# Turning the queries of one batch by DMA instead of on TensorE, and moving a VectorE reduction to an earlier step, in a sparse attention and gated feed-forward kernel

## The chip, the cores and the metric

The kernel runs on one core of a Trainium2 chip. The metric is the time of one execution on the device in microseconds (us), lower is better. Engines: PE is TensorE (PEld its weight loads), DVE is VectorE, ACT is ScalarE, POOL is GpSimd, SP is SyncE, which here only issues transfers. Each execution also reports the mean clock that was granted to PE, as a share of full speed.

## The reference, cut to what matters

Four batches of attention (8 heads, 768 tokens, head size 64). A query sees its neighbours within 16 tokens and one summary of each block of 32 keys: the elementwise maximum of the keys, and the mean of the values. The result, 3072 tokens of width 512, goes through a gated feed-forward layer.

```
k_sum = k.reshape(B, H, nb, 32, D).max(axis=3)
v_sum = v.reshape(B, H, nb, 32, D).mean(axis=3)
scores_l = where(|i - j| < 16, q @ k.T / sqrt(D), -1e9)
scores_s = q @ k_sum.T / sqrt(D) + log(32)
x = softmax([scores_l, scores_s]) @ [v, v_sum]          # 3072 x 512
out = x + sigmoid(x @ w_res) * ((gelu(x @ w_gate) * (x @ w_val)) @ w_out)
```

## The kernel before

The work is cut into eight units of half a batch (384 tokens), 0 to 7; unit u belongs to batch u // 2. A unit has two stretches. In the first, twelve "fo steps" each compute one 128-row slice of the hidden layer: four g matmuls and four vv matmuls on PE, a GELU on ACT, a product gvT on DVE. The second is the output part (r and f matmuls), and PE starts it with the scores s of the *next* unit; their exp runs on ACT, the mask product on DVE (P), and PE's ao matmuls need the masked P. So at the end of a unit ACT, DVE and PE hand work to each other at close quarters.

Batch data for the next batch are prepared in the shadow of the fo steps. For batches 2 and 3, q and k are loaded token by token (`q_nat`, `k_nat`) and turned to head-by-token order by a transposing DMA (`turn_q`, `turn_k`). For batch 1, q was loaded in another order (`q_sb`, four tokens to a partition) and turned on PE, with a copy by ACT, in eight `q_step`s. The maxima over key blocks (`k_blocks`) are DVE work for every batch. POOL copies the block means of v into place (`vsum_bc`).

```python
def load_q(b, half):                      # 4 tokens to a partition: 96 x 8 runs
    t = qk.tile([QP, H, QJ, D], BF16, tag=f"q_sb{half}", name="q_sb")
    nc.gpsimd.dma_start(out=t.rearrange("p h j d -> p h (j d)"), in_=q[b, :, ...])

def load_q_nat(b):                        # token order: 6 transfers of 128 x 8 runs
    for c in range(NQ):
        nc.gpsimd.dma_start(out=q_nat[:, c]..., in_=q[b, :, c * 128:(c + 1) * 128, :]...)

def turn_q(b, half):
    cs = slice(half * NSUB, (half + 1) * NSUB)
    nc.sync.dma_start_transpose(out=qT[b % 2][:, cs]..., in_=q_nat[:, cs]...)

def k_blocks(b, hp):
    kw = kW[b % 2][:, :, hp]
    ks = work.tile([128, NB], BF16, tag="ks", name="ks")
    nc.vector.tensor_reduce(out=ks..., in_=kw[:, :, 0:QT]..., axis=X, op=ALU.max)       # L205
    nc.vector.tensor_copy(kw[:, :, BAND:BAND + NB], ks....to_broadcast([128, NT, NB]))  # L209

def vsum_bc(b, lo, hi, eng):              # called four times with three tiles each, on POOL
    eng.tensor_copy(vext[b % 2][96:128, lo:hi, :, 0:D], src)                            # L263

# ... (cut) the main loop, u = unit, nb = next batch, half = u % 2
for fo in range(...):
    fo_step(st, gvT, fo)
    if u == 0 and fo >= 8:
        q_step(0, 1, fo - 8, ps_t, "t")
    if u == 2 and fo < NP:
        q_step(1, 1, fo, ps_t, "t")
    # ... (cut)
    if half == 1 and nb < B:
        # ... (cut)
        if fo == (4 if nb == 1 else 1):
            vsum_grp(nb, ps_t, "t")
            for i in range(4):
                vsum_bc(nb, 3 * i, 3 * i + 3, nc.gpsimd)
            if nb > 1:
                turn_q(nb, 0); turn_q(nb, 1)
        if nb == 1:
            if fo < NP:
                k_step(nb, fo, ps_t, "t")
            elif 7 <= fo < 7 + NP:
                q_step(nb, 0, fo - 7, ps_t, "t")
        elif 8 <= fo < 8 + NP:
            k_blocks(nb, fo - 8)

# the output part, which begins with the scores of unit n = u + 1
def mid_out(u, st, gvT, nst):
    s_step(n, 0, nst); res_step(st, 0); ffn_step(st, gvT, 0, 0, 2)
    s_step(n, 1, nst); ffn_step(st, gvT, 0, 2, 6)
    av_step(n, 0, nst)                    # ao: needs the masked P of s_step(n, 0)
    # ... (cut)
```

The softmax here doesn't subtract the row's maximum and nothing guards it: scores larger than these inputs give would overflow.

## Time and profile before

| | before |
|---|---|
| time, median of 3 | 277.61 us (275.67 to 278.51) |
| the profiled execution | 275.43 us, span of the trace 273.5 us |
| PE busy | 257.3 us, 94% of the span |

The profile page of the kernel before. The first line gives busy time per engine. The second part cuts the span into 40 slices; PEclk is the granted PE clock in tenths. The last line is the start of the part on the chain of work that ended last.

```profile
PE 257.3 (94%) x2280; PEld 138.6 (51%) x2305; DVE 155.3 (57%) x341; ACT 128.6 (47%) x204; POOL 103.4 (38%) x140
...
PE   7889988999989999999979999999989999999994
...
PEclk9999999999999999999999999999999999999999
DMA  5999999999002999949902899969802410130003
...
PE 74%; DMA 11%; DVE 5%; POOL 4%; issue 3%; ACT 1%; POOLq 0%; DVEq 0%
```

PE is the bottleneck: over 90% busy in almost every slice. The slices with a digit below 9 lie in the start-up (to about 48 us), at the ends of units 1, 3 and 5 (slices 11, 20 and 29, counted from 0) and at the very end. DMA is busy throughout until 68 us (slices 0 to 9); after that it has pauses.

PE's waits in the kernel before, longest first (total us, times, longest us):

```profile
PE ao L291 <- DVE P L280: 2.7, 2, 1.6
PE s L273 <- ACT P L277: 1.6, 2, 1.1
```

Both concern the end of units. Where they come from is seen in the timeline. First, the end of unit 1 (columns: start, duration, engine, line, operation, output<-input, shapes, and in brackets the idle time before it and what ended that):

```profile
77.34 0.36 PE L230 MATMUL tp<-ident,q_sb 96*64 96x96 bf16 x8
...
77.64 0.35 PE L273 MATMUL s<-qT,kW 64*128 64x64 bf16 x12
77.75 0.48 ACT L232 COPY qT<-tp 128x384 bf16<-128x384 bf16 x1 [1.11 <-PE tp L230]
...
78.25 1.28 ACT L277 ACT_TABLE_LOAD   x1
...
79.54 0.90 ACT L277 ACTIVATE P<-s,bias_t 128x768 bf16<-128x768 f32 x1
...
80.49 0.29 PE L273 MATMUL s<-qT,kW 64*128 64x64 bf16 x8 [1.10 <-ACT P L277]
```

The last q step stands between the last vv and the scores. ACT's copy of it (0.48 us) comes before the reload of its table (1.28 us), so the exp P starts at 79.54, and the second group of scores, which needs the score buffer, waits 1.10 us.

Second, the end of unit 3 (DVE, POOL and the PE instruction that waited):

```profile
135.72 5.70 POOL L263 COPY vext<-vsum 32x1536 bf16<-32x1536 bf16 x4 [8.34 <-DMA vsum<-vpart]
...
136.91 0.37 DVE L209 COPY kW<-ks 128x288 bf16<-128x288 bf16 x1
...
138.63 1.46 DVE L209 COPY kW<-ks 128x288 bf16<-128x288 bf16 x1
...
141.91 0.23 DVE L209 COPY kW<-ks 128x288 bf16<-128x288 bf16 x1
...
143.19 1.02 DVE L280 TENSOR_TENSOR P<-P,maskt 128x768 bf16<-128x768 bf16 x2
...
143.80 0.38 PE L291 MATMUL ao<-vext,P 128*64 128x65 bf16 x12 [1.61 <-DVE P L280]
```

The key block steps sit between the last gvT products and the mask product P. One of the four copies L209 takes 1.46 us where a later one takes 0.23: it overlaps POOL's four copies L263, which run back to back from 135.72 to 141.42, 1.43 us apart. PE waits 1.61 us for the masked P.

### The profile page before, as it was taken

How to read it: one execution, taken by the hardware profiler on the slowest of the kernel's cores; microseconds unless marked ns; L12 is line 12 of the kernel's file. 1: busy time of each engine (PE TensorE's matmuls, PEld its weight loads, DVE VectorE, ACT ScalarE, POOL GpSimd, SP SyncE). 2: the span in 40 equal slices, each digit the busy share in tenths (PEclk: the TensorE clock that was granted, in tenths of full speed). 3: DMA queues.
4: the chain of work that ended last, by engine and by line, in shares of the span. 5: the costliest groups of instructions: out<-in, count | busy, mean ns of one | idle time of the engine just before them, and what ended most of it. 6: DMA issues, size and time to landing. Idle time of an engine off the chain costs nothing.

```text
span 273.5 us, 5780 instructions
## 1 busy us (share of the span) xinstructions
PE 257.3 (94%) x2280; PEld 138.6 (51%) x2305; DVE 155.3 (57%) x341; ACT 128.6 (47%) x204; POOL 103.4 (38%) x140
## 2 busy tenths in 40 slices
PE   7889988999989999999979999999989999999994
PEld 2445643555544555445634565445634565456543
DVE  5857432499427534665597644665597544764424
ACT  1776346565473555733363436633462437443320
POOL 8795574260340796216160697054520000000000
PEclk9999999999999999999999999999999999999999
DMA  5999999999002999949902899969802410130003
GB/s 88 172 107 188 196 209 201 183 149 172 10 0 46 159 143 133 87 120 134 163 4 43 136 155 132 117 119 154 134 0 49 135 18 2 39 112 25 0 2 115
DMA packets 100074, 28.37 MB, mean 104 GB/s; under 512 B 83912, under 2 KB 97056, under 8 KB 100048
## 3 DMA queue, kind: packets, MB, share of 16 engines
q0 software_dynamic: 63760, 14.87, 60.1%
q1 hardware_dynamic: 36288, 13.14, 23.9%
q8 instruction: 18, 0.29, 0.5%
q14 instruction: 8, 0.07, 0.1%
HBM read 29.36 MB, written 6.29 MB: 130 GB/s over the span
## 4 chain that ended last, share of the span: by engine, by line
PE 74%; DMA 11%; DVE 5%; POOL 4%; issue 3%; ACT 1%; POOLq 0%; DVEq 0%
PE f L365 20%; PE g L317 20%; PE vv L317 19%; PE r L355 6%; DMA w_out<-in_moe_w_out_dram 4%; DMA w_val<-in_moe_w_val_dram 4%; PE ao L291 3%; DMA q_sb<-in_q_dram 3%; PE s L273 2%; DVE ks L205 2%; POOL vext L105 1%; DVE gvT L323 1%; POOL w_gate L182 1%; PE f L389 1%; PE tp L230 1%
## 5 line engine op out<-in xcount | busy, mean ns | idle before, releaser
L323 DVE TENSOR_TENSOR gvT<-ge,vv 128x384 bf16<-128x384 f32 x96 | 52.8, 552 | 62.1 <-PE vv L317 59.5
L322 ACT ACTIVATE ge<-g 128x384 f32<-128x384 f32 x96 | 47.0, 490 | 68.9 <-DVE gvT L323 44.5
L317 PE MATMUL g<-xT,w_gate 128*128 128x384 bf16 x384 | 78.6, 326 | 0.1
L317 PE MATMUL vv<-xT,w_val 128*128 128x384 bf16 x384 | 78.4, 326 | 0.2 <-DVE gvT L323 0.2
L365 PE MATMUL f<-w_out,gvT 128*128 128x512 bf16 x262 | 64.8, 380 | 1.4 <-DMA w_out<-in_moe_w_out_dram 1.0
L317 PEld LDWEIGHTS <-w_val 128*128 128x128 bf16 x384 | 37.5, 98 | 25.5 <-issue 0.8
L317 PEld LDWEIGHTS <-w_gate 128*128 128x128 bf16 x384 | 36.1, 98 | 25.1 <-issue 1.3
L365 PEld LDWEIGHTS <-gvT 128*128 128x128 bf16 x276 | 24.8, 98 | 28.2 <-DMA w_out<-in_moe_w_out_dram 1.5
L277 ACT ACTIVATE P<-s,bias_t 128x768 bf16<-128x768 f32 x32 | 28.8, 901 | 19.8 <-PE s L273 19.2
L105 POOL DMA_DIRECT2D vext<-in_v_dram x48 | 32.9, 745 | 10.8 <-DMA w_out<-in_moe_w_out_dram 4.6
L263 POOL COPY vext<-vsum 32x1536 bf16<-32x1536 bf16 x14 | 20.0, 1464 | 28.7 <-DMA vsum<-vpart 28.6
L280 DVE TENSOR_TENSOR P<-P,maskt 128x768 bf16<-128x768 bf16 x32 | 17.6, 557 | 19.8 <-ACT P L277 18.1
L371 DVE SCALAR_TENSOR_TENSOR th<-th,f 128x512 f32<-128x512 f32 (+1 forms) x25 | 16.5, 660 | 17.5 <-PE f L365 17.2
L358 ACT ACTIVATE th<-r 128x512 f32<-128x512 f32 x24 | 14.2, 595 | 26.1 <-PE r L355 26.0
L355 PE MATMUL r<-w_res,xT 128*128 128x512 bf16 x88 | 23.8, 380 | 1.5 <-issue 1.0
L297 DVE TENSOR_TENSOR xn<-ao,rz 128x384 bf16<-128x384 f32 x32 | 17.8, 557 | 1.3 <-DVE rz L295 0.2
L374 DVE SCALAR_TENSOR_TENSOR o<-th,xn 128x512 f32<-128x512 f32 (+1 forms) x25 | 16.8, 670 | 0.9
L291 PEld LDWEIGHTS <-P 128*64 128x64 bf16 x384 | 8.7, 110 | 16.4 <-issue 6.6
L118 POOL DMA_DIRECT2D k_nat<-in_k_dram x24 | 16.4, 740 | 0.3 <-issue 0.3
L205 DVE TENSOR_REDUCE ks<-kW 128x24 bf16<-128x768 bf16 x16 | 15.1, 942 | 1.5 <-ACT kW L220 1.4
L291 PE MATMUL ao<-vext,P 128*64 128x65 bf16 x384 | 12.1, 199 | 3.5 <-DVE P L280 2.7
L355 PEld LDWEIGHTS <-xT 128*128 128x128 bf16 x96 | 8.8, 98 | 9.2
(71 smaller groups left out, 167.0 us busy)
## 6 DMA issues: line engine op xcount, KB each, us to landing
out_dram<-o SPq DMA_DIRECT2D x23, 256.0 KB, 2.3
vext<-in_v_dram POOLq DMA_DIRECT2D x48, 64.0 KB, 6.2
q_sb<-in_q_dram POOLq DMA_DIRECT2D x4, 384.0 KB, 9.6
w_gate<-in_moe_w_gate_dram POOLq DMA_DIRECT2D x6, 256.0 KB, 9.8
w_val<-in_moe_w_val_dram POOLq DMA_DIRECT2D x6, 256.0 KB, 10.3
w_out<-in_moe_w_out_dram POOLq DMA_DIRECT2D x3, 512.0 KB, 13.0
k_nat<-in_k_dram POOLq DMA_DIRECT2D x24, 64.0 KB, 4.3
q_nat<-in_q_dram POOLq DMA_DIRECT2D x12, 128.0 KB, 5.8
```

The costliest lines, as they stand in the source:

```text
L105: nc.gpsimd.dma_start(out=vext[b % 2][0:QT, t, :, 0:D], in_=v[b, :, t * QT:(t + 1) * QT, :].rearrange("h p d -> p h d"))
L205: nc.vector.tensor_reduce(out=ks.rearrange("d (t n) -> d t n", n=2), in_=kw[:, :, 0:QT].rearrange("d t (n w) -> d t n w", w=BLK), axis=myb ...
L263: eng.tensor_copy(vext[b % 2][96:128, lo:hi, :, 0:D], src)
L277: nc.scalar.activation(P.rearrange("p a t q -> p a (t q)"), s[:, :, 0:TU], AF.Exp, scale=scale, bias=bias_t[:])
L280: nc.vector.tensor_mul(Pf, Pf, maskt.unsqueeze(1).to_broadcast([128, 2 * HT, QT]))
L291: nc.tensor.matmul(ao[64 * e:64 * e + 64, sub, hh, :], P[:, hh, t, :], vext[b % 2][:, half * HT + t, 2 * hp + hh, 0:D + 1], start=True, st ...
L297: nc.vector.tensor_mul(xn, ao[:, :, :, 0:D], rz.to_broadcast([128, NSUB, 2, D]))
L317: nc.tensor.matmul(ps[:, 0:TU], w[:, ko, fo * 128:(fo + 1) * 128], st["xT"][:, ko, :], start=(ko == 0), stop=(ko == KO - 1), skip_group_ch ...
L322: nc.scalar.activation(ge[:], g[:, 0:TU], AF.Gelu)
L323: nc.vector.tensor_mul(gvT[:, fo, :], ge[:], vv[:, 0:TU])
L355: nc.tensor.matmul(r[:], st["xT"][:, ko, ss], w_res[:, ko, :], start=(ko == 0), stop=(ko == KO - 1))
L365: nc.tensor.matmul(st["f", sub][:], gvT[:, fo, ss], w_out[:, fo, :], start=(fo == 0), stop=(fo == FO - 1), skip_group_check=True)
```

## The change

The intent: take the eight q steps of batch 1 off PE and ACT by loading q of batch 1 the way batches 2 and 3 do, and take the key block steps away from the crowded end of units 3 and 5.

```diff
             if half == 0 and nb == 1:
                 k_sb[nb] = load_qk(k, nb, 1, "k_sb")
                 v_loads(nb)
-                for i in range(2):
-                    q_sb[2 * nb + i] = load_q(nb, i)
+                load_q_nat(nb)
@@ ...
-                if u == 2 and fo < NP:
-                    q_step(1, 1, fo, ps_t, "t")
@@ ...
-                        if nb > 1:
-                            turn_q(nb, 0)
-                            turn_q(nb, 1)
+                        turn_q(nb, 0)
+                        turn_q(nb, 1)
                     if nb == 1:
                         if fo < NP:
                             k_step(nb, fo, ps_t, "t")
-                        elif 7 <= fo < 7 + NP:
-                            q_step(nb, 0, fo - 7, ps_t, "t")
-                    elif 8 <= fo < 8 + NP:
-                        k_blocks(nb, fo - 8)
+                    elif 2 <= fo < 2 + NP:
+                        k_blocks(nb, fo - 2)
```

## The prediction

> **What bounds the kernel now.** TensorE: on the page, PE is busy 257.3 of 273.5 us (94%) at full clock; the chain that ended last is 74% PE. The rest is a DMA-bound start-up (to about 45 us), untouched here, and short PE gaps at unit ends. A unit is half a batch: 12 fo steps of 1.30 us (g, vv), then the output part, beginning with the next unit's scores.
>
> **What it removes.**
> 1. Eight q steps (64 PE transposes, 8 PSUM copies of 0.48 us on ACT). By the PE timeline an fo step with one takes 1.69 us, not 1.30: 0.39 us each. Unit 2 holds four: 1.6 us. Unit 1 holds three inside its fo loop: 1.2 us.
> 2. The fourth in unit 1 stands before the output part; its ACT copy delays the table load and the first exp, and PE waits 1.10 us for P. From the last eight vv matmuls' start to the second r group: 8.39 us in unit 1, 6.93 in unit 2, which has none: 1.46 us.
> 3. Key block maxima at fo 8 to 11 (0.94 us reduce, 0.23 us copy each) leave DVE behind at the end of units 3 and 5. The same stretch takes 8.60 and 8.44 us there, PE waiting up to 1.61 us for the masked P: 1.67 + 1.51 us. Two of those copies took 1.46 and 1.42 us, ending with a POOL copy of the value means. The Trainium skill, "SBUF — State Buffer", section "Who interferes with whom", says a two-port DVE copy and a GpSimd operation exclude each other for a whole instruction; this trace agrees. At fo 2 to 5 POOL is idle.
>
> Sum: about 7.4 us, nearly all on the critical path (PE).
>
> **What it adds.**
> - DVE at fo 2 to 5: gvT, reduce and copy start 1.61 us apart against PE's 1.30, so gvT lags 0.3 us more a step, 1.2 us at fo 6. With four PSUM buffers vv tolerates about 1.2 us. Cost: 0 to 0.4 us a unit. The turned keys land near 115 us, ten early.
> - Loads of q of batch 1: six issues of 0.90 us on POOL for two of 0.81, 6144 packets for 1536. In unit 3 the same six drain in about 10 us; the two old loads took about 7. So the queue, full to about 68 us now, stays full to 71 to 73. The vsum transfers (issued 68.3 to 71.3) land at 72.7 now, perhaps 1 to 2 us later. The first turn goes out near 71.5 to 72 and takes 3.8 us: about 75.5. The scores need it near 76.1 (77.34 less 1.2). Little slack; POOL's copies of the means also meet the first masked P. I allow 0.8 us overall.
>
> **Prediction.** 277.6 - 7.4 + 0.8 = 271.0 us (268.8 to 274.2, 8 in 10). Faster by over 2%: 0.64; within: 0.34; slower: 0.02.
>
> **What would show it.** All fo steps of unit 2 at 1.30 us; the end stretch of units 1, 3 and 5 near 6.9 us; no PE wait for DVE at fo 4 to 8 of units 3 and 5; s of unit 2 not waiting for the turned q; PE busy about 3 us less, ACT 3.8.
>
> **What would make it wrong.** The turned q, or the means, land late in unit 1, and the s or ao matmuls wait (each us late costs a us); gvT's backlog exceeds the PSUM slack; POOL's copies block the masked P in units 1 and 3; or the 1% spread hides part.

## The result, and the profile after

The kernel after takes 268.45 us in the median (268.17 to 268.99, 4 runs), against 277.65 us for the kernel before (4 runs). The ratio is 0.9681, with a 95% interval of 0.9627 to 0.9734. Here and below a ratio is the mean time of one kernel's fast runs over that of the other's fast runs of the same rounds, so not quite the ratio of the medians quoted. Executions over 1.5% slower than the fastest of the same kernel are left out of the means. The result is faster than the predicted range (268.8 to 274.2) reached.

The page of the kernel after (the same parts, without the DMA line):

```profile
PE 257.7 (97%) x2241; PEld 138.5 (52%) x2241; DVE 154.4 (58%) x341; ACT 124.8 (47%) x196; POOL 107.0 (40%) x144
...
PE   8897999999999999999999999999999999999994
...
PEclk9997999999999999999999999999999999999999
...
PE 89%; DMA 7%; DVE 1%; POOL 1%; issue 1%; ACT 1%; POOLq 0%
```

PE is at 97% and is 89% of the chain, against 74%. The digits below 9 after the start-up are gone. PE's clock fell in the fourth slice (the 7), in the start-up; more on that below. PE's busy time itself did not fall (257.3 and 257.7 us): the trace of the kernel before lacks some matmul records (262 f matmuls against 276 after, 88 r against 96), so this sum can't be compared. The tp group of the q steps can: 5.8 us before, 2.9 after.

PE's waits in the kernel after:

```profile
PE ao L291 <- DMA vext<-vext: 1.5, 1, 1.5
...
PE ao L291 <- DVE vext L244: 0.7, 1, 0.7
PE s L273 <- ACT P L277: 0.5, 1, 0.5
```

What is left of over 0.2 us comes before 22 us, in the start-up. The wait for the masked P is gone from the list.

The end of unit 1 after:

```profile
75.93 1.28 ACT L277 ACT_TABLE_LOAD   x1
...
76.62 0.35 PE L273 MATMUL s<-qT,kW 64*128 64x64 bf16 x12
...
77.23 0.90 ACT L277 ACTIVATE P<-s,bias_t 128x768 bf16<-128x768 f32 x1
...
78.16 1.36 DVE L280 TENSOR_TENSOR P<-P,maskt 128x768 bf16<-128x768 bf16 x1 [0.81 <-ACT P L277]
...
78.30 0.35 PE L273 MATMUL s<-qT,kW 64*128 64x64 bf16 x12
```

The table load now starts before the scores, and the second group of scores waits for nothing. The mask product at 78.16 took 1.36 us instead of 0.56, because POOL copies the means at that time; PE has enough f matmuls in between and hardly noticed.

The fo steps 2 to 5 of unit 3 after (DVE, and POOL's first copy of the means):

```profile
123.91 0.56 DVE L323 TENSOR_TENSOR gvT<-ge,vv 128x384 bf16<-128x384 f32 x1 [0.69 <-PE vv L317]
...
125.36 0.23 DVE L209 COPY kW<-ks 128x288 bf16<-128x288 bf16 x1
...
125.51 0.55 DVE L323 TENSOR_TENSOR gvT<-ge,vv 128x384 bf16<-128x384 f32 x1
...
130.14 0.23 DVE L209 COPY kW<-ks 128x288 bf16<-128x288 bf16 x1
130.29 1.01 DVE L323 TENSOR_TENSOR gvT<-ge,vv 128x384 bf16<-128x384 f32 x2
130.30 1.46 POOL L263 COPY vext<-vsum 32x1536 bf16<-32x1536 bf16 x1 [6.81 <-ACT ge L322]
```

The gvT products start 1.59 to 1.60 us apart here, PE's fo steps are 1.30 us apart, so DVE falls behind by 0.3 us a step, as predicted, and PE never waits for it. All four copies L209 take 0.23 us, and the last is over just as POOL begins.

The time from one unit's first scores to the next unit's, in us, read from the PE timelines. Interval u goes from s of unit u to s of unit u + 1, so it holds the output part of unit u - 1 and the fo steps of unit u:

| interval | before | after | less |
|---|---|---|---|
| 2 (end of unit 1, fo steps of unit 2) | 31.72 | 28.99 | 2.73 |
| 3 | 29.82 | 29.82 | 0 |
| 4 (end of unit 3) | 30.64 | 28.96 | 1.68 |
| 5 (its last fo steps hold key blocks before) | 30.23 | 29.83 | 0.40 |
| 6 (end of unit 5) | 30.08 | 28.96 | 1.12 |

Interval 2, with the three q steps and the fourth before the scores of unit 2 (3 x 0.39 + 0.30 = 1.47 us), gives 4.2 us for the q part. Intervals 4 to 6 give 3.2 us for the key block part. Together that is 7.4 us, the sum of the prediction. The start-up of the traced execution after was 0.46 us later (first g matmul of unit 1 at 57.55 instead of 57.09 us), hence 7.0 us between the spans, 273.5 and 266.5. But the medians differ by 9.2 us. The traced execution of the kernel before, 275.43 us, was its fastest of five; the one after, 268.17 us, also its fastest, but only 0.3 us below its median. So the question: what do most executions of the kernel before lose that the traced one did not, and which part of the change removes it?

### The profile page after: what moved, and what is told of

The parts are those of the page before. It is cut to its first block, busy times and chain, and to the rows that moved or that the text cites. A ratio compares the mean times of both kernels' runs of the same rounds, so it can differ in the third digit from the quotient of the medians.

```text
span 266.5 us, 5683 instructions
## 1 busy us (share of the span) xinstructions
PE 257.7 (97%) x2241; PEld 138.5 (52%) x2241; DVE 154.4 (58%) x341; ACT 124.8 (47%) x196; POOL 107.0 (40%) x144
## 4 chain that ended last, share of the span: by engine, by line
PE 89%; DMA 7%; DVE 1%; POOL 1%; issue 1%; ACT 1%; POOLq 0%
PE g L317 24%; PE vv L317 24%; PE f L365 23%; PE r L355 8%; PE ao L291 4%; PE s L273 3%; DMA q_sb<-in_q_dram 3%; DMA vext<-vext 2%; DMA vext<-in_v_dram 1%; PE f L389 1%; PE vs L251 1%; PE xp L302 1%; PE tp L198 1%; POOL k_sb L90 0%; PE tp L230 0%
## 5 line engine op out<-in xcount | busy, mean ns | idle before, releaser
L365 PE MATMUL f<-w_out,gvT 128*128 128x512 bf16 x276 | 67.7, 380 | 0.0
L317 PEld LDWEIGHTS <-w_gate 128*128 128x128 bf16 x384 | 36.8, 98 | 25.6 <-issue 1.3
L280 DVE TENSOR_TENSOR P<-P,maskt 128x768 bf16<-128x768 bf16 x32 | 19.0, 595 | 20.4 <-ACT P L277 18.6
L123 POOL DMA_DIRECT2D q_nat<-in_q_dram x18 | 15.9, 924 | 0.7 <-issue 0.7
```

The costliest lines, as they stand in the source:

```text
L280: nc.vector.tensor_mul(Pf, Pf, maskt.unsqueeze(1).to_broadcast([128, 2 * HT, QT]))
L317: nc.tensor.matmul(ps[:, 0:TU], w[:, ko, fo * 128:(fo + 1) * 128], st["xT"][:, ko, :], start=(ko == 0), stop=(ko == KO - 1), skip_group_ch ...
L365: nc.tensor.matmul(st["f", sub][:], gvT[:, fo, ss], w_out[:, fo, :], start=(fo == 0), stop=(fo == FO - 1), skip_group_check=True)
```

## The experiments

All gave correct results. Theories: **A**, the DVE copies of the key block maxima wait for POOL's copies (the exclusion that the prediction cites) by an amount that changes from execution to execution. **B**, the excess is in the start-up, whose transfers land sooner or later by chance. **C**, PE's granted clock falls after a PE gap. Each call ran the kernel before beside its own kernels; its fast runs had means of 277.26, 277.54, 277.17 and 277.55 us in the four calls, so the kernel before repeats to some 0.4 us between calls, which ran on different chips. A kernel's own runs scatter more: the 95% intervals below are about 0.4% (1.1 us) to either side, so a difference of two kernels of different calls is known to about 1 us at best.

### The parts alone, a control, and a copy that does not wait

b_again is the kernel before. k_only has only the second part of the diff (`2 <= fo < 2 + NP`), q_only only the first part. b_nolock is the kernel before with

```diff
-            nc.vector.tensor_copy(kw[:, :, BAND:BAND + NB], ks.unsqueeze(1).to_broadcast([128, NT, NB]))
+            if b < 2:
+                ... # (cut: the copy as it was)
+            else:
+                nc.vector.tensor_reduce(out=kw[:, :, BAND:BAND + NB],
+                                        in_=ks.unsqueeze(2).unsqueeze(1).to_broadcast([128, NT, NB, 1]),
+                                        axis=mybir.AxisListType.X, op=ALU.max)
```

> The kernel before, unchanged, as a control and for a second trace. The first trace (execution of 275.43 us, span 273.5) is the fastest of five executions; the others took 275.7 to 278.5. Theory A (the 2 us that the trace does not show come from more DVE copies of key block maxima waiting for POOL's copies of the means in units 3 and 5): where the traced execution takes 277 us or more, more than two of the eight copies last over 1 us, or PE waits longer there, and the start of unit 1 stays near 57 us. Theory B (start-up transfers): a slow execution is late already at the start of unit 1 (57.0 us in the first trace), by the whole excess. Median 277.0 expected, ratio 1.00.

> Only the key block maxima moved to fo 2 to 5; q as before. From the first trace: 1.67 + 1.51 us less, so 3.2 us if only the traced waits go (ratio 0.9885). Theory A: the missing 2 us belong to this part, so about 5 us (ratio 0.982), and the spread of the runs shrinks below 1 us. Theory B: 3.2 us, and the spread stays near 3 us.

> Only q of batch 1 in token order and turned by DMA; key block maxima at fo 8 to 11 as before. From the first trace 1.2 + 1.46 + 1.6 = 4.3 us less (ratio 0.9845). Theory A: 4.3 us, and the spread of the before kernel (about 3 us) stays, as the key blocks still meet POOL's copies. A theory that the q part is worth more than counted: 6 us or more (ratio 0.978).

> The kernel before, with the copy of the key block maxima of batches 2 and 3 into the key tile done as a tensor_reduce over one element (same values, same place at fo 8 to 11, DVE still, but a form that should not take the port that POOL holds), about 0.4 to 0.5 us instead of 0.23. If the port wait is most of the end-of-unit loss (and of the spread): no such instruction over 0.6 us, end stretch of units 3 and 5 shorter by about 1 us each, ratio 0.990 or lower, spread under 1 us. If DVE's own backlog of reduce work is the loss: ratio 0.998 to 1.003, as eight instructions grow by 0.2 us each.

| run | median, us | range | ratio to before | 95% |
|---|---|---|---|---|
| b_again | 276.64 | 275.52 to 278.06 | 0.9984 | 0.9942 to 1.0026 |
| k_only | 272.58 | 272.15 to 273.90 | 0.9833 | 0.9797 to 0.9869 |
| q_only | 273.25 | 270.32 to 274.44 | 0.9827 | 0.9779 to 0.9875 |
| b_nolock | 275.22 | 274.71 to 277.52 | 0.9947 | 0.9904 to 0.9990 |

The key block part is worth 4.6 us alone (0.0167 x 277.3), where the trace gave 3.2 (the interval of its ratio reaches from 3.6 to 5.6 us). The q part is worth 4.8 us alone (0.0173 x 277.3), together 9.4, near the 9.2 us of both at once. With the key blocks moved the spread is 1.75 us; where they stay at fo 8 to 11 it is 2.5 to 4.1 us. The gain speaks for A. The spread doesn't settle it: A had expected under 1 us for k_only, and for b_nolock, whose copy should not wait, under 1 us and a ratio of 0.990 or lower; b_nolock came out at 0.9947 with a spread of 2.8 us. B is at work as well: the first scores of unit 2 came at 77.64 in the first trace, at 78.56 in b_again and at 80.53 in b_nolock, where PE had waited 2.88 us for the rims of v (rows of a tile's neighbours that the tile also needs, copied from vext to vext).

In the trace of q_only a third thing showed. PE after the gap at the end of unit 5:

```profile
197.87 1.04 PE L365 MATMUL f<-w_out,gvT 128*128 128x512 bf16 x4
200.64 0.38 PE L291 MATMUL ao<-vext,P 128*64 128x65 bf16 x12 [1.74 <-DVE P L280]
...
201.24 2.29 PE L365 MATMUL f<-w_out,gvT 128*128 128x512 bf16 x5
203.45 0.54 PE L291 MATMUL ao<-vext,P 128*64 128x65 bf16 x12
```

Five f matmuls took 2.29 us; four before the gap took 1.04, so five take about 1.25. In the same trace, stretches of 2 us with the busy time per engine (the third column from the right is the granted PE clock):

```profile
200.00:202.00 2.00, 1.36 (x26) 0.76 (x27) 1.81 (x5) 0.66 (x1) 0.00 (x0) 0.82 0.03 8
202.00:204.00 2.00, 2.00 (x20) 0.78 (x20) 0.56 (x1) 0.25 (x1) 0.00 (x0) 0.50 0.24 49
204.00:206.00 2.00, 1.69 (x28) 0.96 (x29) 1.31 (x3) 1.09 (x2) 0.00 (x0) 0.82 0.00 0
```

After an idle stretch of 1.74 us the clock fell to 0.50 for about 3.4 us (the shortfalls 0.18, 0.50 and 0.18 of 2 us each make 1.72 us lost), and this cost about 1.5 us on top of the wait (the sum further below). Hence theory C. The Trainium skill, "TensorE: Matmul & The Clock Gate", Part 1, names this: a clock gate that lets half of the pulses pass once an activity window of about 3.4 us was idle, the windows running free of the program. The length of the slow stretch agrees; the gap that set it off was shorter.

### Dummy matmuls in the gaps, a split of the q part, and the slack of fo 2 to 5

b_fill puts five dummy matmuls before the ao matmuls at the ends of units 3 and 5. a_fill_start is the kernel after with six more dummies in the start-up. b_q_early moves the q steps of unit 1 from fo 7 to 10 to fo 6 to 9. a_k_double does each key block step of the kernel after twice.

```diff
# b_fill, in mid_out
             ffn_step(st, gvT, 0, 2, 6)
+            if u in (3, 5):
+                wq = ps_t.tile([128, 512], F32, tag="t", name="wq")
+                for _ in range(5):
+                    nc.tensor.matmul(wq[:], warm[:, 0:128], warm[:], start=True, stop=True)
             av_step(n, 0, nst)
# a_fill_start
-        fill(3)
+        fill(9)
         av_step(0, 0, st, ps_mm, "mm")
# b_q_early
-                        elif 7 <= fo < 7 + NP:
-                            q_step(nb, 0, fo - 7, ps_t, "t")
+                        elif 6 <= fo < 6 + NP:
+                            q_step(nb, 0, fo - 6, ps_t, "t")
# a_k_double
                         k_blocks(nb, fo - 2)
+                        k_blocks(nb, fo - 2)
```

> The kernel before, with five dummy matmuls (about 0.22 us each at full clock, 1.1 us together) put where PE waits for the masked P at the ends of units 3 and 5. The DVE work and its port waits stay. Theory C: a PE gap of 1.5 to 1.7 us there sometimes lets the granted clock fall to half for about 3 us, as the trace of the q part alone shows after a gap of 1.74 us (the five f matmuls after it took 2.29 us instead of 1.25); this is what makes most executions of the kernel before slower than the traced one. Then: the runs' mean clocks rise (fewer below 0.990), the median falls by 1 to 1.5 us to about 275.9 (ratio 0.995 to 0.996), the fastest runs stay at 275.5. Theory A (only waits of DVE for the port): nothing changes, ratio 0.999 to 1.001, low clocks as often as before.

> The kernel after, with six more dummy matmuls (1.3 us) in the start-up before the first ao group, where PE waited 1.48 us for the value rims in the traced execution and then ran at half clock for some 3.4 us. If the half clock there costs time in the end: no clock below 0.997, median 267.5 to 268.0. If the start-up is bound by the weights' transfers anyway (the kernel before lost nothing by it but waited later for w_out): 268.4, within 0.3 us. Where the rims come early the six matmuls cost up to 1 us at that point.

> The kernel before with the q steps of the first half of batch 1 one fo step earlier in unit 1 (6 to 9 instead of 7 to 10), so that none stands between the last vv and the scores; nothing is loaded or turned otherwise. By the prediction's second item the last q step's copy delays the table load: PE's wait of 1.10 us for P in the scores of unit 2 goes, ratio 0.996 (-1.1 us). If that wait had another cause: ratio 0.999 to 1.001, and the wait of 1.10 us is still there in the trace.

> The kernel after, with each key block step at fo 2 to 5 of units 3 and 5 done twice (same values; 4.7 us more DVE work per unit). gvT then falls behind by about 1.5 us a step instead of 0.3, so the PSUM buffers run out at the second step: PE waits about 1.2 us per step from then on, some 3.5 to 5 us per unit, so 275 to 278 us if the slack is the 1.2 us that the prediction gave. If PE hides it (no PE wait for DVE in these steps): 268.5.

| run | median, us | range | ratio to before | 95% |
|---|---|---|---|---|
| b_fill | 277.61 | 275.84 to 278.91 | 0.9993 | 0.9936 to 1.0051 |
| a_fill_start | 267.90 | 267.34 to 268.59 | 0.9655 | 0.9607 to 0.9703 |
| b_q_early | 275.77 | 274.49 to 278.63 | 0.9939 | 0.9877 to 1.0000 |
| a_k_double | 281.21 | 278.89 to 282.40 | 1.0112 | 1.0047 to 1.0177 |

b_fill moved nothing: C is not the main cause. In its trace the copies L209 waited longer than in the first one, and PE waited 1.05 and 0.79 us although 1.1 us of dummies had been put in the gaps.

b_q_early: interval 2 fell from 31.72 to 30.55 us and the wait of 1.10 us is gone from its trace. So the last q step's place did cause it, as the prediction's second item said. The time agrees but is no proof by itself: the interval of its ratio ends at 1.0000.

a_k_double shows how little slack there was. PE waited 0.23, 2.64 and 1.86 us for gvT in unit 3; the second of these waits, and the group after it:

```profile
134.16 0.81 PE L317 MATMUL vv<-xT,w_val 128*128 128x384 bf16 x4 [2.64 <-DVE gvT L323]
134.81 1.44 PE L317 MATMUL g<-xT,w_gate 128*128 128x384 bf16 x4
```

It cost 12.7 us (281.21 less the 268.5 of the kernel after), more than the 7 to 10 us expected. Two things add to the backlog: the steps run on into POOL's copies (DVE copies L209 of 1.33 and 1.46 us in that trace), and the clock falls after the gap, as seen by g groups of four taking 1.44 instead of 0.81 us. In unit 3 the gvT products started 2.73 us apart (124.00, 126.73, 129.46), so gvT lagged by 1.4 us after one double step, which cost PE nothing, and by 2.9 us after two, when PE first waited, 0.23 us. PE's slack against gvT lies between these two, by an estimate from that first wait near 2.6 us: about twice the 1.2 us that the prediction gave.

a_fill_start: the mean clocks rose to 0.997 and above in all six runs (0.990 to 0.999 in the four runs of the kernel after).

### The start-up filled

With the start-up filled, less of its luck is in the comparison. b_fs is the kernel before with `fill(9)`; b_fs_endfill has seven dummies at the ends of units 3 and 5 besides; a_again is the kernel after; a_fs_again the kernel after with `fill(9)`.

> The kernel before with six more dummy matmuls in the start-up, as in the filled kernel after; this takes most of the spread that comes from late value rims and the half clock behind them out of the runs, so that what is left comes from the ends of units 3 and 5. There, five traces so far fit: loss of a unit = 0.35 us + the sum of the port waits of its four copies (1.1 to 1.9 us) + 1.6 us where the clock fell after the gap (seen once, after a gap of 1.74 us). Theory C: some runs still have clocks near 0.994 or 0.988 (one or two windows of 3.4 us at half clock) and these are the slow ones; fastest 275.0, slowest 278, median about 276.5. Theory A alone: all clocks above 0.996 and a spread under 1.5 us.

> The same, with seven dummy matmuls (1.5 us) at the ends of units 3 and 5 besides, so that PE does not sit idle there for 1.5 us at a stretch. Theory C: clocks above 0.996 in all runs, slowest runs gone, median 275.5 to 276.0, about 0.7 us below its neighbour without them. Theory A alone: same as the neighbour within 0.3 us.

> The kernel after, unchanged, in the same rounds: 268.5 us median, spread under 1.5 us, clocks 0.990 to 1.0. Theory C says that it can lose clock only in the start-up, since no PE wait over 0.5 us is left after it.

> The kernel after with the six dummy matmuls in the start-up, in the same rounds as the kernel after: 267.9 us, 0.5 us below it, clocks above 0.996. If the difference seen between two calls was chance or another chip: no difference.

| run | median, us | range | mean of fast runs | ratio to before | 95% |
|---|---|---|---|---|---|
| b_fs | 276.38 | 275.83 to 278.96 | 276.71 | 0.9989 | 0.9938 to 1.0040 |
| b_fs_endfill | 277.39 | 276.53 to 279.68 | 277.56 | 1.0013 | 0.9966 to 1.0061 |
| a_again | 268.72 | 268.16 to 269.94 | 268.87 | 0.9700 | 0.9659 to 0.9741 |
| a_fs_again | 267.54 | 267.40 to 268.26 | 267.64 | 0.9656 | 0.9618 to 0.9694 |

b_fs had clocks of 0.997 and above in five of six runs, and these five took 275.8 to 276.6 us; the sixth, at 0.990, took 278.96. So the clock still falls now and then; that it fell at the end of a unit in that run is likely but not shown, since only the trace of q_only caught such a fall. Leaving a_k_double aside, seven traces of unfilled kernels lost clock: q_only at the end of unit 5, the other six in the start-up. Filling the ends (b_fs_endfill) made nothing faster, and one of its runs still had a clock of 0.981; C's expectation failed again. a_again spread by 1.8 us with clocks down to 0.985, where under 1.5 us and 0.990 had been expected.

The filled kernel after is the fastest kernel: 267.64 against 268.87 us in the same rounds (means), a ratio of 0.9954. Why, is seen in the start-up of the two traces. Without the dummies:

```profile
18.42 0.82 PE L422 MATMUL wp<-warm 128*128 128x512 bf16 x3
...
22.49 0.35 PE L291 MATMUL ao<-vext,P 128*64 128x65 bf16 x11 [2.35 <-DMA vext<-vext]
...
24.26 0.54 PE L291 MATMUL ao<-vext,P 128*64 128x65 bf16 x12
```

With them:

```profile
18.58 2.12 PE L422 MATMUL wp<-warm 128*128 128x512 bf16 x8
20.62 0.38 PE L291 MATMUL ao<-vext,P 128*64 128x65 bf16 x12
...
22.27 0.38 PE L291 MATMUL ao<-vext,P 128*64 128x65 bf16 x12
```

Twelve ao matmuls take 0.38 us at full clock and 0.54 after the wait of 2.35 us for the rims (a transfer from vext to vext). With the nine dummies of `fill(9)` in that place (eight are in the trace), PE stays busy and the clock stays up. But in this second trace the rims also landed earlier, before 20.62, where PE did not wait for them. The trace of b_fs shows the same dummies where the rims came late:

```profile
22.34 0.35 PE L291 MATMUL ao<-vext,P 128*64 128x65 bf16 x11 [1.44 <-DMA vext<-vext]
...
23.96 0.38 PE L291 MATMUL ao<-vext,P 128*64 128x65 bf16 x12
```

It waited 1.44 us after the dummies and kept a clock of 1.00; in the trace of the kernel after, without them, PE waited 0.71 and then 1.48 us at this place, and its clock fell to 0.50 behind that.

### The two parts once more, and the wait of the copies taken away in two ways

By now the traces allowed a sum, the time lost at the end of a unit (the expectations below round its first term to 0.35 us). The loss of intervals 4 to 6 against the 28.96, 29.83 and 28.96 us of the kernel after, beside the excess of the four copies L209 over 0.235 us ("port waits"):

| trace, end of unit | port waits | loss | loss less waits |
|---|---|---|---|
| before, 3 and 5 | 1.36, 1.19 | 1.68, 1.52 | 0.32, 0.33 |
| b_again, 3 and 5 | 1.27, 1.09 | 1.60, 1.41 | 0.33, 0.32 |
| q_only, 3 | 1.23 | 1.56 | 0.33 |
| q_only, 5 (clock fell) | 1.49 | 3.32 | 1.83 |
| b_fs, 3 and 5 | 1.42, 1.61 | 1.74, 1.93 | 0.32, 0.32 |

So in these traces a unit's loss is 0.33 us for the DVE work itself, plus the port waits, plus some 1.5 us where the clock falls. The waits differ between executions of the same code: up to the end of unit 3, b_fill is the kernel before and b_fs_endfill is b_fs, and the waits of that unit summed to 1.36, 1.27 (b_again) and 1.88 us, and to 1.42 and 2.47 us. Four more kernels test this, all with the filled start-up: k_fs and q_fs are k_only and q_only; b_fs_nolock has the reduce in place of the copy; b_fs_small cuts POOL's copies of batches 2 and 3 from four to twelve:

```diff
-                        for i in range(4):
-                            vsum_bc(nb, 3 * i, 3 * i + 3, nc.gpsimd)
+                        m = 3 if nb == 1 else 1
+                        for i in range(NT // m):
+                            vsum_bc(nb, m * i, m * i + m, nc.gpsimd)
```

> The kernel before with the filled start-up and the key block maxima at fo 2 to 5; q as before. If the key block part is worth 3.2 us, 273.5 (from 276.7, the mean of the filled kernel before); if 4.5 us, 272.2. The q part's fixed PE time of 4.1 us would put it 4.1 us above the filled kernel after (267.6), so at 271.8; that is what I expect, with a spread under 1 us.

> The filled start-up and q of batch 1 by DMA; key block maxima at fo 8 to 11. 4.1 us below the filled kernel before: 272.6. If the key block part varies by phase, the spread is 2 us or more here and under 1 us in the kernel with the blocks at fo 2 to 5.

> The filled kernel before, with the copy of the maxima of batches 2 and 3 as a reduce over one element. By the sum found so far (0.35 us + port waits + clock losses a unit), each unit loses 0.35 + 4 x 0.22 = 1.2 us and no more in every run: 271.8 + 2.4 = 274.2, spread under 1 us. If the port waits are not the excess: 276 or more.

> The filled kernel before, with POOL's four copies of the means (1.46 us each, three tiles) of batches 2 and 3 cut into twelve (one tile each, about 0.5 us). A DVE copy that waits for the end of one POOL instruction then waits 0.5 us at most, not 1.2: no DVE copy of the maxima above 0.8 us in the trace, median 275.0 to 275.8. If the wait lasts until POOL is done with all of them: copies as long as before or longer, 276.5 or more.

| run | median, us | range | mean of fast runs | ratio to before | 95% |
|---|---|---|---|---|---|
| k_fs | 272.17 | 271.57 to 272.90 | 272.25 | 0.9805 | 0.9765 to 0.9845 |
| q_fs | 273.30 | 271.58 to 276.47 | 272.72 | 0.9832 | 0.9781 to 0.9883 |
| b_fs_nolock | 274.64 | 274.24 to 275.87 | 274.78 | 0.9896 | 0.9855 to 0.9937 |
| b_fs_small | 273.88 | 273.13 to 275.10 | 274.04 | 0.9869 | 0.9827 to 0.9912 |

(In q_fs's trace the same sum holds: waits of 1.92 and 1.57 us, losses of 2.26 and 1.90. One run, 276.47 us at a clock of 0.986, is in the median and the range, not in the mean.)

The q part: 276.71 less 272.72 is 4.0 us, and 272.25 less 267.64 is 4.6 us. The key block part: 276.71 less 272.25 is 4.5 us, and 272.72 less 267.64 is 5.1 us. These are differences between calls; the ratios to the kernel before of the same call give 4.4 and 4.1 us for q, 5.1 and 4.9 us for the key blocks. k_fs came out 0.4 us slower than the 271.8 us expected.

b_fs_nolock should lose 0.33 + 4 x 0.22 = 1.2 us a unit against k_fs, whatever POOL does. That was put as 271.8 + 2.4 = 274.2; with the measured k_fs, known only afterwards, it is 272.25 + 2.4 = 274.65, and 274.78 was measured, with five of six runs within 0.7 us of each other. In the trace of b_nolock these reduces ran beside POOL's four copies (137.50 to 143.18) and took no longer:

```profile
139.81 0.45 DVE L212 TENSOR_REDUCE kW<-ks 128x288 bf16<-128x288 bf16 x1
...
141.62 0.45 DVE L212 TENSOR_REDUCE kW<-ks 128x288 bf16<-128x288 bf16 x1
```

b_fs_small was faster than expected (275.0 to 275.8). It lost 0.95 and 0.82 us a unit in its trace, where the port waits sum to 0.63 and 0.49 us (0.32 and 0.33 left over): 272.25 + 1.77 = 274.02, measured 274.04, again a sum made afterwards. Its DVE copies at the end of unit 3, beside POOL copies of 0.61 us:

```profile
136.72 0.62 DVE L209 COPY kW<-ks 128x288 bf16<-128x288 bf16 x1
...
138.69 0.31 DVE L209 COPY kW<-ks 128x288 bf16<-128x288 bf16 x1
```

So a DVE copy waits for the end of the POOL instruction in flight, not of all of them. With the same DVE work in the same place and only POOL's instructions made shorter, the kernel gained 2.7 us (276.71 to 274.04; 3.3 by the ratios, whose intervals do not overlap). In the two traces the waits fell by 1.9 us (3.03 to 1.12). That settles the waits for POOL, A's mechanism, as the largest part of what the key blocks cost. The size is less settled.

What stays open: in the untraced runs of the unfilled kernel before, how much of the excess is port waits, how much the clock's fall at the ends of units and how much the start-up. The traces of b_fs and k_fs give 3.4 us for the key block part (3.67 less 0.27), their means 4.5. The other traces narrow this. In the eight traces with the key blocks at fo 8 to 11, as copies, and POOL's long copies, intervals 4 to 6 lost 3.0 to 4.9 us, 3.9 on average, against 3.2 in the first trace. And B has a share: five traces run the same code up to the first scores of unit 2 (before, b_again, k_only, b_fill, b_nolock), and these came at 77.64, 78.56, 79.27, 79.54 and 80.53 us, so the first trace also had the earliest start-up. The slowest of them, b_fill's execution of 278.25 us, is 2.8 us above the first: 1.9 us by its start-up and 0.95 us by longer port waits (its dummies cost nothing in the sum). Whether the q part of the change also moves the start-up can't be told: with the 1.47 us of its q steps added, the three unfilled traces of the kernel after and of a_k_double reached that point at 78.1 to 78.7 us, inside the same spread.

## Why the prediction was right or wrong

The time, 268.45 us, lies just outside the range. The mechanisms named were right, two sizes were not.

- **PE bounds the kernel, and the end stretches lose time:** right. PE went from 94% to 97%, from 74% to 89% of the chain, and its waits for P are gone.
- **The q part, items 1 and 2, 4.3 us:** right. 4.2 us in the traces, 4.0 to 4.8 us in the runs; all fo steps of unit 2 took 1.30 us, and b_q_early showed the 1.10 us wait to come from the last q step's place.
- **The key block part, item 3, 1.67 + 1.51 us:** wrong in size. The first pair of traces repeats it (3.2 us), but the runs gave 4.5 to 5.1 us, and eight traces 3.9 us on average. The step that failed is "277.6 - 7.4", in its term 1.67 + 1.51: a saving read in one execution, the fastest (275.43), was taken off a median of slower ones. The prediction saw the two copies of 1.46 and 1.42 us and named the exclusion of DVE and POOL, but treated those waits as fixed. They change with where the two instruction streams happen to meet; over the kernels with POOL's long copies a unit's waits summed to between 1.1 and 1.9 us, in b_fs_endfill once to 2.5, and the long gap they open let the clock fall for another 1.5 us in one trace (q_only). Of the 1.3 to 1.9 us that the runs gained beyond the prediction's 3.2, the eight traces show 0.7; the rest is open.
- **"I allow 0.8 us overall":** wrong, it cost nothing. The transfers did not come late: DMA, which the prediction kept full to 71 to 73 us, showed a share of 0.03 in the stretch 70 to 72 us of the trace after. The first turn went out at 72.20 us, after SP's transfers of the means, close to what was expected (71.5 to 72), and the scores at 76.62 us did not wait for it. The means came 0.75 us later than before, by just as much as their own issue. POOL's copies did meet the masked P of unit 1 (1.36 us instead of 0.56), inside PE's slack.
- **gvT's backlog, 0 to 0.4 us a unit:** 0. The lag of 0.3 us a step is as predicted, and PE did not wait. a_k_double shows that a step twice as heavy does stall it, and that the slack was more than the 1.2 us given.
- **PE busy about 3 us less:** could not be read, since records are missing in the trace before. ACT fell by 3.8 us (128.6 to 124.8), as said.

Together: 0.8 us of allowance not needed and 1.3 to 1.9 us more from the key blocks make 2.1 to 2.7 us, and the prediction missed the median by 2.6 us. That the two sizes fit the miss so well is partly luck, since the differences that they come from are known to about 1 us.

## What to carry to other kernels

Where an engine's instruction can be held up by another engine's, the loss is a matter of phase: take several traces, or read the spread of the runs, before taking it for a constant, and don't subtract a saving seen in the fastest execution from a median. A crowded hand-over between engines is a bad place for work that can run anywhere; if it can't be moved, another form of the instruction, or shorter instructions on the other engine, recovers a good part (1.9 and 2.7 of 4.5 us here, between calls). And a PE gap can cost twice, once as a wait and once as a slower clock after it: where PE has to wait for a transfer anyway, dummy matmuls there can be worth more than they cost (1.2 us in the kernel after; the 0.5 us in the kernel before lie within the noise), but at the ends of units they gained nothing.

## What the Trainium skill lacked or had wrong

- "TensorE: Matmul & The Clock Gate", Part 1, says that PE falls to half clock after an idle window of about 3.4 us, in free-running windows, and the table in its section "Why this matters for your kernels" asks for no idle gaps over about 3 us. Half clock it was, and for about 3.4 us (0.82, 0.50, 0.82 in three stretches of 2 us). But a continuous gap of 1.74 us was enough in the trace of q_only, while gaps of 2.19 us (q_fs) and 1.87 us (b_fs) were not followed by it. A rule of 3 us is too wide for this kernel: of these three gaps below it one was followed by the fall. That would fit free-running windows, but no run here tests it.
- "SBUF — State Buffer", "Who interferes with whom", is confirmed by three numbers and contradicted by none: DVE copies of 0.23 us took up to 1.46 us beside POOL copies of 1.46 us and up to 0.65 us beside POOL copies of 0.61 us; the reduce, which the page says never contends on trn2, stayed at 0.45 us; the mask product with two inputs in SBUF grew from 0.56 to 1.36 us. What it lacks is that such a wait varies between executions of the same code (at the end of unit 3: 1.27, 1.36 and 1.88 us in the kernel before, 1.42 and 2.47 us in the filled one), and that shortening the GpSimd instruction is a remedy (2.7 us here).
- No page says how far the landing of an SBUF to SBUF transfer beside a full load queue varies: PE waited between 0 and 2.9 us for the same rims in the ten traces without the fill.
